# Values loaded by GpSimd's queue with the cast in the transfer, and causal masks two blocks at a time

## The chip, the cores and the metric

The kernel runs on one core of a Trainium2 chip. The core has a matrix engine (TensorE, PE in the profile; its weight loads are PEld), VectorE (DVE), ScalarE (ACT), GpSimd (POOL) and SyncE (SP), which here only issues transfers. Every engine works through its own instructions in program order and waits on semaphores for the others. Sixteen DMA engines move data between memory and the core's buffer; a transfer is issued by an instruction in the queue of SP, ACT or POOL. The metric is the device time of one execution in microseconds (us).

## The reference

The program is selective attention followed by a block with layer norm and a two-layer network. There are 8 batches, 8 heads, 576 positions, 64 elements per head.

```python
scores = scale * q @ k.T                       # per batch and head, 576 x 576
cum = cumsum(max(s, 0))                        # per batch and head
scores = where(causal, -1e9, scores + minimum(-(cum[i] - cum[j]), 0))
attn = softmax(scores)
x = attn @ v                                   # heads side by side: (8, 576, 512)
xn = (x - mean) / sqrt(var + 1e-6) * g_ln
out = x + max(xn @ w_ch1, 0) @ w_ch2           # 512 -> 2048 -> 512
```

All inputs are float32 in memory, and so is the output.

## The kernel before

The work is a sequence of 64 heads, numbered n = 8 b + h over batch b and head h. The 576 positions are cut into four tiles of 128 and one of 64. For each head, `scores` (L344) computes transposed score blocks on PE into three banks, sa, sb and sc; ACT takes the exponential of each bank into the tile `er` (four heads deep, in bfloat16). The 64 x 64 corner blocks of two heads are done together in `scores_d` (L381). From head 10 on, the causal mask is applied on POOL after the exponentials: `affine_select` (L371) zeroes one half of each of the four 128 x 128 diagonal blocks of a head, and one more (L401) does the corners of two heads. `pv` (L419) then multiplies the masked exponentials with the values, 15 matmuls into the bank `pot`. The values lie in `v_bf`, two buffers that batches take in turns, with a column of ones that gives the sum of each row; `pv_norm` divides by it on DVE.

Between these, PE runs the two-layer network of the previous batch in units of four matmuls (`mlp1`, L533, and `mlp2`, L551), taken from a list (`queue`) by `run_units`. The first 18 heads are ordered by a written list of steps (`PLAN`, L946); from head 18 on a loop (L974) does, for every n: `pre(n)`, `scores`, units, `scores_d` for even heads, units, then `pv` of head n-2, then more units. So the pot of a head runs two heads later than its scores.

`pre(n)` (L852) holds the loads for later heads. Keys and queries are taken in groups of four heads (gam, two per batch). From group 5 on, `ld_rows` (L187) issues two loads per tile on SP's queue into a staging tile; `cast_rows` (L200) casts that tile on POOL and copies the bias columns; `tr_rows` (L210) issues a DMA transpose on SP's queue into `kq`, from which PE reads. For a group these steps come six to three heads ahead of its first head. The staging tiles (pool `stage`, six buffers) are shared by the row tiles and the value tiles.

Values of batches 0 and 1 are loaded by POOL's queue in the prologue, straight into `v_bf`, with the cast from float32 to bfloat16 in the transfer (`ld_cast_v`, L173). For batches 2 to 7, `pre(n)` calls `ld_v` (L162), which loads one tile of v in float32 into a staging tile on SP's queue, and one head later `cast_v` (L180), which casts it on POOL into `v_bf`. For batch nb the five tiles are loaded at heads n = 8 nb - 7 to 8 nb - 3 (for batch 2: 11 to 15) and cast one head later. Within `pre(n)` the value steps come behind the steps for rows, and the masks of head n come behind `pre(n)` on POOL. The weights (`w1_bf`, `w2_bf`) and the pairs of keys and queries of early groups also come by POOL's queue, in the prologue and at heads 11 and 12. Finished rows of the output are stored by SP's queue at the end of a `mlp2` quarter.

Of the kernel before, what the change touches and what calls it, by code (L numbers as in the profile page):

```python
# [9 lines left out]
F32 = mybir.dt.float32  # L10
# [5 lines left out]
P = 128  # L16
# [3 lines left out]
def kernel(  # L20
# [11 lines left out]
    nc = tc.nc  # L32
    B, H, S, D = q.shape
# [5 lines left out]
    NF = S // P  # L39
    NT = NF + 1  # L40
    TL = S - NF * P
# [3 lines left out]
    OB, OC, OD = 512, 1024, 1536  # L45
# [11 lines left out]
    stage = ctx.enter_context(tc.tile_pool(name="stage", bufs=6))  # L57
# [25 lines left out]
    v_bf = [const.tile([P, NT, H, D + 1], BF16, name=f"v_bf{i}") for i in range(2)]  # L83
# [27 lines left out]
    def copy_on(eng, out, in_):  # L111
        if eng == "act":
            nc.scalar.copy(out=out, in_=in_)
        elif eng == "dve":
            nc.vector.tensor_copy(out=out, in_=in_)
        else:
            nc.gpsimd.tensor_copy(out=out, in_=in_)  # L117


    loaded = {}  # L120
# [37 lines left out]
    def ld_cast_pair(g):  # L158
        ld_cast("k", g)
        ld_cast("q", g)  # L160

    def ld_v(b, t):  # L162
        if b >= B:
            return
        pn = P if t < NF else TL
        tmp = stage.tile([P, H, D], F32, name="vtmp", tag="st")
        nc.sync.dma_start(
            out=tmp[:pn], in_=v[b, :, t * P : t * P + pn, :].rearrange("h s d -> s h d")
        )
        loaded["v", b, t] = tmp  # L170


    def ld_cast_v(b, t):  # L173
        pn = P if t < NF else TL
        nc.gpsimd.dma_start(
            out=v_bf[b % 2][:pn, t, :, 0:D],
            in_=v[b, :, t * P : t * P + pn, :].rearrange("h s d -> s h d"),
        )

    def cast_v(b, t, eng):  # L180
        if b >= B:
            return
        pn = P if t < NF else TL
        copy_on(eng, v_bf[b % 2][:pn, t, :, 0:D], loaded.pop(("v", b, t))[:pn])


    def ld_rows(gam, t):  # L187
        pn = P if t < NF else TL
# [39 lines left out]
    def ld_w2(i):  # L228
        nc.gpsimd.dma_start(
            out=w2_bf[:, 4 * i : 4 * i + 4, :], in_=w2_r[:, 4 * i : 4 * i + 4, :]  # L230
        )
# [89 lines left out]
    def k_cols(b, h, kb):  # L321
        i, hh = home(b * 2 + h // G), h % G
        if b * 2 + h // G < NPE:
            return kq[i][0:KA, 0, hh, kb * P : (kb + 1) * P]
        n = P if kb < NF else TL
        o = kb * 2 * G * P + hh * n
        return kq[i].rearrange("p u h s -> p (u h s)")[0:KA, o : o + P]

    def q_cols(b, h, q0, q1):
        i, hh = home(b * 2 + h // G), h % G  # L330
        if b * 2 + h // G < NPE:
            return [(q0, q1, kq[i][0:KA, 1, hh, q0:q1])]
        flat = kq[i].rearrange("p u h s -> p (u h s)")
        full = flat[0:KA, 0 : NF * 2 * G * P].rearrange("p (t h s) -> p t h s", t=NF, s=P)
        o = NF * 2 * G * P + (G + hh) * TL
        got = []
        if q0 < NF * P:
            qf = min(q1, NF * P)
            got.append((q0, qf, full[:, q0 // P : qf // P, G + hh, :]))
        if q1 > NF * P:  # L340
            got.append((NF * P, q1, flat[0:KA, o : o + TL]))
        return got

    def scores(b, h):  # L344
        e = er[:, h % 4, :]
        pe_mask = b * H + h < NM

        def bank(name, blocks, o):
            a = ps_s.tile([P, 512], F32, name=name, tag="s")
            for c, kb, q0, q1, diag in blocks:  # L350
                for a0, a1, cols in q_cols(b, h, q0, q1):
                    nc.tensor.matmul(  # L352
                        a[:, c + a0 - q0 : c + a1 - q0],
                        lhsT=k_cols(b, h, kb),
                        rhs=cols,
                        start=True,
                        stop=not (pe_mask and diag),
                    )
                if pe_mask and diag:
                    nc.tensor.matmul(  # L360
                        a[:, c : c + P], lhsT=ident, rhs=maskT, start=False, stop=True
                    )
            nc.scalar.activation(out=e[:, o : o + 512], in_=a, func=ACT.Exp, scale=scale)  # L363

        bank("sa", ((0, 0, 0, 512, True),), 0)
        bank("sb", ((0, 0, 512, 576, False), (64, 1, 128, 576, True)), OB)
        bank("sc", ((0, 2, 256, 576, True), (320, 3, 384, 576, True)), OC)
        if pe_mask:
            return
        for o in (0, OB + 64, OC, OC + 320):  # L370
            nc.gpsimd.affine_select(  # L371
                out=e[:, o : o + P],
                in_=e[:, o : o + P],
                compare_op=ALU.is_ge,
                fill=0.0,
                base=0,
                pattern=[[1, P]],
                channel_multiplier=-1,
            )

# [79 lines left out]
    st = {}  # L460
# [168 lines left out]
    for i in range(2):  # L629
# [9 lines left out]
        out=maskT,  # L639
        in_=maskT,  # L640
# [3 lines left out]
        pattern=[[1, P]],  # L644
# [207 lines left out]
    def pre(n):  # L852
        if n == 14:
            for r in rows:
                nc.gpsimd.memset(r[:, :, :, KA:P], 0.0)
        if n in PAIR_LOADS:
            ld_cast_pair(PAIR_LOADS[n])
        if n in (11, 12):
            ld_w2(n - 9)
        if n in (8, 9):  # L860
            aug(n - 5, nc.sync)
        for gam in range(NPE, NG):
            m = n - 4 * gam
            if m == -6:
                ld_rows(gam, 0), ld_rows(gam, 1)
            elif m == -5:
                cast_rows(gam, 0), cast_rows(gam, 1)
                ld_rows(gam, 2), ld_rows(gam, 3)
            elif m == -4:
                tr_rows(gam, 0), tr_rows(gam, 1)  # L870
                cast_rows(gam, 2), cast_rows(gam, 3)
                ld_rows(gam, 4)
            elif m == -3:
                tr_rows(gam, 2), tr_rows(gam, 3)
                cast_rows(gam, 4)
                tr_rows(gam, 4)
        for nb in range(2, B):
            m = n - H * nb + (5 if nb == 2 else 7)
            if 0 <= m < NT:
                ld_v(nb, m)  # L880
            if 1 <= m <= NT:
                cast_v(nb, m - 1, "pool")

    def pv_next():
        pb, ph_ = pend.pop(0)
# [4 lines left out]
        if ph_ == 7:  # L890
# [8 lines left out]
            out=c_in[:, 0:P], in0=c_in[:, 0:P], scalar=0.0, in1=eight, op0=ALU.max, op1=ALU.mult  # L899
# [24 lines left out]
            out=c_in[:, P:S], in_=c_in[:, P:S], func=ACT.Relu, scale=1.0 / scale  # L924
# [16 lines left out]
        "U": lambda: run_units(1, True),  # L941
        "u": lambda: run_units(1),
        "p": lambda n: pre(n),
    }

# [21 lines left out]
    for word in PLAN.split():  # L967
        step, _, eng = word.partition(":")
# [5 lines left out]
    for n in range(2 * H + 2, BH):  # L974
        b, h = n // H, n % H
# [65 lines left out]
```

## Time and profile before

| | |
|---|---|
| median of three runs | 362.97 us (362.14 to 363.56) |
| the profiled execution, its own time | 361.1 us |
| its span (first to last instruction) | 359.4 us |
| PE busy | 348.9 us, 97% |
| DVE, ACT, POOL busy | 199.1, 187.5, 169.6 us |
| masks on POOL (L371) | 216 instructions, 59.0 us |
| casts of v on POOL (L117) | 30 instructions, 18.3 us |
| casts and copies of rows on POOL (L204, L205) | 110 instructions, 45.0 us |
| v loads issued on SP (L167) | 30, median 596 ns to issue |
| v loads issued on POOL in the prologue (L175) | 10, median 928 ns to issue |
| read from memory, written to it | 37.11 MB, 9.44 MB |

How to read the views. A row of a group gives a line of the kernel, an engine, an operation, output and inputs by name, their shapes, how many there were, their busy time and the mean length of one, and how long the engine sat idle just before them, with what ended most of that. In a view in order of time, a line gives the start in us, the length, the engine, and the same names; instructions of one kind that follow each other are merged (x15), and a bracket tells how long the engine idled before and what released it. A view by stretches gives, for each stretch, the busy time of PE, PEld, DVE, ACT and POOL with their instruction counts, PE's granted clock, the mean busy share of the DMA engines and the GB/s that they moved. Matmuls are pipelined, so their lengths overlap; the step from one group's start to the next is the time that PE gives to it. An instruction that issues a transfer counts as no busy time of its engine in the page's first row.

### The profile page before, as it was taken

The page shows a single profiled execution, that of the slowest core. Times are in us where ns is not written, and L with a number is a line of the kernel's source. Part 1 is how long each engine was busy: PE and PEld are TensorE (multiplying, and loading weights), DVE is VectorE, ACT ScalarE, POOL GpSimd, SP SyncE. Part 2 cuts the span into 40 slices and gives each one's busy share as a digit, 9 for nine tenths or more (in the row PEclk, how much of TensorE's full clock was granted, in tenths as well). Part 3 has the DMA queues.
Part 4 walks back from the last instruction along what each step waited for, and adds up shares of the span by engine and source line. Part 5 has one row for each costly group of instructions (what it writes and reads, how often), then busy time and mean ns, then how long its engine had stood idle before and what let it go on. Part 6 is the DMA issues. An engine that isn't in the chain of part 4 may idle for free.

```text
span 359.4 us, 8530 instructions
## 1 busy us (share of the span) xinstructions
PE 348.9 (97%) x3144; PEld 200.8 (56%) x3190; DVE 199.1 (55%) x540; ACT 187.5 (52%) x363; POOL 169.6 (47%) x451
## 2 busy tenths in 40 slices
PE   7999999989999999999999999999999999999995
PEld 3899665545555555555555555555555554444444
DVE  7787888924476536844484539543855482113111
ACT  4899886557524763367326743575247432501500
POOL 9996768456666562464745473537422110000000
PEclk9999999999999999999999999999999999999999
DMA  9999999999899998599889885999610011011013
GB/s 151 173 186 172 201 196 202 184 215 210 183 161 257 201 167 176 143 208 178 187 194 206 193 179 116 247 170 182 139 60 2 2 58 59 2 58 58 0 33 88
DMA packets 164202, 52.09 MB, mean 145 GB/s; under 512 B 152848, under 2 KB 159552, under 8 KB 164160
## 3 DMA queue, kind: packets, MB, share of 16 engines
q1 hardware_dynamic: 139248, 42.43, 56.3%
q0 software_dynamic: 23472, 8.33, 20.6%
q10 hardware_dynamic: 1440, 0.79, 0.9%
q8 instruction: 25, 0.41, 0.5%
q14 instruction: 17, 0.14, 0.1%
HBM read 37.11 MB, written 9.44 MB: 130 GB/s over the span
## 4 chain that ended last, share of the span: by engine, by line
PE 85%; DVE 5%; DMA 3%; POOL 2%; issue 2%; SPq 1%; POOLq 0%; DVEq 0%
PE ph L537 32%; PE py L555 27%; PE pot L429 6%; PE sc L352 3%; PE sb L352 3%; PE sa L352 3%; PE ph L817 2%; PE trx L522 2%; PE st L715 2%; DMA rowtmp<-in_q_dram 2%; DVE xn L504 2%; PE pot L773 1%; PE trt L693 1%; DMA c_in<-in_s_dram 1%; DMA kq<-kq 1%
## 5 line engine op out<-in xcount | busy, mean ns | idle before, releaser
L555 PE MATMUL py<-w_bf,hT 128*128 128x512 bf16 (+1 forms) x565 | 132.5, 373 | 1.5 <-DVE yo L564 0.4
L537 PE MATMUL ph<-xT,w_bf 128*128 128x512 bf16 x462 | 113.0, 379 | 1.1 <-DVE yo L564 0.2
L547 ACT ACTIVATE hT<-ph 128x512 bf16<-128x512 f32 x100 | 59.6, 597 | 65.2 <-PE ph L537 65.2
L555 PEld LDWEIGHTS <-hT 128*128 128x128 bf16 x592 | 53.4, 98 | 48.8 <-issue 0.9
L537 PEld LDWEIGHTS <-w_bf 128*128 128x128 bf16 x544 | 48.6, 97 | 49.9 <-issue 2.9
L363 ACT ACTIVATE er<-sa 128x512 bf16<-128x512 f32 x56 | 33.4, 596 | 66.0 <-PE sa L352 42.1
L371 POOL TENSOR_SCALAR_AFFINE_SELECT er<-er 128x128 bf16<-128x128 bf16 x216 | 59.0, 298 | 18.6 <-ACT er L363 18.4
L545 DVE TENSOR_SCALAR hT<-ph 128x512 bf16<-128x512 f32 x36 | 24.9, 692 | 58.2 <-PE ph L537 57.9
L204 POOL CAST kq<-rowtmp 128x512 bf16<-128x512 f32 (+1 forms) x55 | 33.4, 606 | 38.3 <-DMA rowtmp<-in_q_dram 37.7
L352 PEld LDWEIGHTS <-kq 68*128 68x128 bf16 x412 | 29.9, 97 | 22.4 <-issue 0.5
L429 PEld LDWEIGHTS <-er 128*128 128x128 bf16 x840 | 33.0, 98 | 13.7 <-POOL er L371 1.5
L564 DVE SCALAR_TENSOR_TENSOR yo<-py,rstd,xb 128x512 f32<-128x512 f32 x32 | 24.0, 749 | 24.4 <-PE py L555 17.9
L441 DVE RECIPROCAL rinv<-pot 128x5 f32<-128x5 f32 x56 | 10.7, 191 | 48.1 <-PE pot L429 47.9
L429 PE MATMUL pot<-v_bf,er 128*128 128x65 bf16 x840 | 35.3, 194 | 1.1 <-POOL er L371 1.0
L363 ACT ACTIVATE er<-sc 128x512 bf16<-128x512 f32 x56 | 34.3, 613 | 0.0
L117 POOL CAST v_bf<-vtmp 128x512 bf16<-128x512 f32 (+1 forms) x30 | 18.3, 612 | 32.4 <-DMA vtmp<-in_v_dram 24.6
L363 ACT ACTIVATE er<-sb 128x512 bf16<-128x512 f32 x56 | 33.6, 600 | 0.0
L443 DVE TENSOR_TENSOR xb<-pot,rinv 128x256 f32<-128x256 f32 x56 | 23.8, 425 | 1.9
L483 POOL TENSOR_TENSOR rstd<-rstd,mhalf 128x4 f32<-128x4 f32 (+1 forms) x8 | 8.7, 1091 | 32.7 <-DVE rstd L482 32.7
L504 DVE SCALAR_TENSOR_TENSOR xn<-xb,mv,gb 128x512 bf16<-128x512 f32 x28 | 21.9, 783 | 1.0
L467 DVE BATCH_NORM_STATS2 stats<-xb 128x6 f32<-128x128 f32 (+1 forms) x84 | 21.9, 320 | 0.3
L352 PE MATMUL sc<-kq 68*128 68x256 bf16 (+1 forms) x200 | 21.7, 226 | 0.0
(117 smaller groups left out, 372.6 us busy)
## 6 DMA issues: line engine op xcount, KB each, us to landing
out_dram<-yo SPq DMA_DIRECT2D x32, 256.0 KB
vtmp<-in_v_dram SPq DMA_DIRECT2D x24, 256.0 KB
rowtmp<-in_k_dram SPq DMA_DIRECT2D x44, 128.0 KB
rowtmp<-in_q_dram SPq DMA_DIRECT2D x44, 128.0 KB
w_bf<-in_moe_w_ch_dram POOLq DMA_DIRECT2D x8, 512.0 KB, 9.4
v_bf<-in_v_dram POOLq DMA_DIRECT2D x8, 128.0 KB, 6.2
kq<-kq SPq DMA_TRANSPOSE x55
kp<-in_k_dram POOLq DMA_DIRECT2D x6, 144.0 KB, 8.8
```

What stands on the lines that cost most here:

```text
L204: nc.gpsimd.tensor_copy(out=r[0:pn, :, :, 0:D], in_=loaded.pop(("rows", gam, t))[0:pn])
L352: nc.tensor.matmul(a[:, c + a0 - q0 : c + a1 - q0], lhsT=k_cols(b, h, kb), rhs=cols, start=True, stop=not (pe_mask and diag),)
L363: nc.scalar.activation(out=e[:, o : o + 512], in_=a, func=ACT.Exp, scale=scale)
L371: nc.gpsimd.affine_select(out=e[:, o : o + P], in_=e[:, o : o + P], compare_op=ALU.is_ge, fill=0.0, base=0, pattern=[[1, P]], channel_mult ...
L429: nc.tensor.matmul(pot[:, t, :], lhsT=e[:, o : o + P], rhs=vv[:, kb, h, :], start=(kb == 0), stop=(kb == last),)
L443: nc.vector.tensor_tensor(out=xb[b][:, :, hs], in0=pot[:, 0:NF, 0:D], in1=rinv[:, 0:NF].unsqueeze(2).to_broadcast([P, NF, D]), op=ALU.mult,)
L504: nc.vector.scalar_tensor_tensor(out=xn, in0=tiles[t], scalar=mvs[b][:, t, 0:1] if b > 0 else mean0[:, t : t + 1], in1=gb, op0=ALU.subtrac ...
L537: nc.tensor.matmul(ph, lhsT=w1_bf[:, kd, fb * P : (fb + 1) * P], rhs=xT[:, kd, :], start=(kd == 0), stop=(kd == KD - 1),)
L545: nc.vector.tensor_scalar_max(out=hT[:, fb, :], in0=ph, scalar1=0.0)
L547: nc.scalar.activation(out=hT[:, fb, :], in_=ph, func=ACT.Relu)
L555: nc.tensor.matmul(py[t], lhsT=hT[:, fb, t * P : (t + 1) * P], rhs=w2_bf[:, fb, c0:c1], start=(fb == 0), stop=(fb == FB - 1),)
L564: nc.vector.scalar_tensor_tensor(out=yo, in0=py[t], scalar=rs, in1=x[:, c0:c1], op0=ALU.mult, op1=ALU.add)
```

## The change

The value tiles of batches 2 to 7 no longer pass through a staging tile. `pre(n)` issues their loads on POOL's queue, with the cast in the transfer, two tiles at n = 8 nb - 4 and three at n = 8 nb - 3, by the function that the prologue uses. `ld_v` and `cast_v` go. The four masks of a head become two instructions, each over two diagonal blocks: blocks 0 and 1, which lie 576 columns apart, and blocks 2 and 3, which lie 320 apart.

```diff
-    def ld_v(b, t):
-        if b >= B:
-            return
-        pn = P if t < NF else TL
-        tmp = stage.tile([P, H, D], F32, name="vtmp", tag="st")
-        nc.sync.dma_start(
-            out=tmp[:pn], in_=v[b, :, t * P : t * P + pn, :].rearrange("h s d -> s h d")
-        )
-        loaded["v", b, t] = tmp
...
     def ld_cast_v(b, t):
         pn = P if t < NF else TL
         nc.gpsimd.dma_start(
             out=v_bf[b % 2][:pn, t, :, 0:D],
             in_=v[b, :, t * P : t * P + pn, :].rearrange("h s d -> s h d"),
         )
-
-    def cast_v(b, t, eng):
-        if b >= B:
-            return
-        pn = P if t < NF else TL
-        copy_on(eng, v_bf[b % 2][:pn, t, :, 0:D], loaded.pop(("v", b, t))[:pn])
...
-        for o in (0, OB + 64, OC, OC + 320):
+        for o, step in ((0, OB + 64), (OC, 320)):
+            two = e[:, o : o + 2 * step].rearrange("p (i c) -> p i c", c=step)[:, :, 0:P]
             nc.gpsimd.affine_select(
-                out=e[:, o : o + P],
-                in_=e[:, o : o + P],
+                out=two,
+                in_=two,
                 compare_op=ALU.is_ge,
                 fill=0.0,
                 base=0,
-                pattern=[[1, P]],
+                pattern=[[0, 2], [1, P]],
                 channel_multiplier=-1,
             )
...
         for nb in range(2, B):
-            m = n - H * nb + (5 if nb == 2 else 7)
-            if 0 <= m < NT:
-                ld_v(nb, m)
-            if 1 <= m <= NT:
-                cast_v(nb, m - 1, "pool")
+            for t in {-4: (0, 1), -3: (2, 3, 4)}.get(n - H * nb, ()):
+                ld_cast_v(nb, t)
```

## The prediction

> **What bounds the kernel now.** I read the busy shares first, then the span in forty slices, then busy time by stretches of 10 us, then the order of time of PE, POOL and SP where a stretch stood out, and last the waits. The page:
>
> ```profile
> PE 348.9 (97%) x3144; PEld 200.8 (56%) x3190; DVE 199.1 (55%) x540; ACT 187.5 (52%) x363; POOL 169.6 (47%) x451
> PEclk9999999999999999999999999999999999999999
> L117 POOL CAST v_bf<-vtmp 128x512 bf16<-128x512 f32 (+1 forms) x30 | 18.3, 612 | 32.4 <-DMA vtmp<-in_v_dram 24.6
> L371 POOL TENSOR_SCALAR_AFFINE_SELECT er<-er 128x128 bf16<-128x128 bf16 x216 | 59.0, 298 | 18.6 <-ACT er L363 18.4
> ```
>
> PE is busy 97% at full clock; 10.5 us of the 359.4 us span are left. An edit on POOL and on the queues takes no work from PE, so it can win only what PE idles, and lose what it makes PE wait. The stretches tell where the idling is:
>
> ```profile
> 0.00:10.00 10.00, 8.09 (x49) 3.72 (x50) 7.29 (x28) 5.25 (x10) 9.25 (x18) 1.00 1.38 152
> ...
> 60.00:70.00 10.00, 9.89 (x88) 5.68 (x89) 9.37 (x25) 6.94 (x14) 7.18 (x19) 1.00 1.04 195
> 70.00:80.00 10.00, 8.69 (x83) 4.89 (x83) 4.13 (x12) 5.37 (x12) 4.41 (x12) 1.00 0.93 208
> 80.00:90.00 10.00, 9.95 (x87) 5.37 (x85) 4.30 (x12) 7.45 (x16) 6.77 (x22) 1.00 1.02 212
> ```
>
> The second number is PE's busy time. Start-up (8.09) and the last stretch (the final output) are out of the change's reach; 70 to 80 is the one stretch in the middle that falls short. There, PE and then POOL in order of time:
>
> ```profile
> 72.53 0.38 PE L352 MATMUL sa<-kq 68*128 68x512 bf16 x1
> 73.11 0.38 PE L352 MATMUL sb<-kq 68*128 68x64 bf16 x3 [0.20 <-DMA kq<-kq]
> ...
> 74.48 1.03 PE L537 MATMUL ph<-xT,w_bf 128*128 128x512 bf16 x4
> 76.50 1.24 PE L429 MATMUL pot<-v_bf,er 128*128 128x65 bf16 x15 [0.99 <-POOL er L371]
> 77.58 1.89 PE L537 MATMUL ph<-xT,w_bf 128*128 128x512 bf16 x7
> ```
>
> ```profile
> 68.48 0.20 POOL L205 COPY kq<-cT 64x32 bf16<-64x32 bf16 x1
> 75.59 0.61 POOL L117 CAST v_bf<-vtmp 128x512 bf16<-128x512 f32 x1 [6.91 <-PE ph L537]
> 76.16 1.03 POOL L371 TENSOR_SCALAR_AFFINE_SELECT er<-er 128x128 bf16<-128x128 bf16 x4
> ```
>
> This is head 18. Its exps ended at 66.1, yet its four masks ran at 76.16, because the first v cast of batch 3 stood ahead of them on POOL. The cast is put down to PE, but its load was issued on SP only at 71.58, behind three transposes (67.24, 4.29 us); the load is the likelier releaser. Steps between PE's groups give the cost. From sa to sb is normally 0.22 us (68.15 to 68.37), here 0.58: 0.36 lost. Four matmuls from 74.48 take 0.86, so pot could start at 75.34 and started at 76.50: 1.16 lost. From pot to the next group is 0.46 elsewhere (81.69 to 82.15), here 1.08: 0.62 lost. Together **2.14 us**. Everywhere else in the middle PE is within 0.3 us of full in every 10 us.
>
> **Part 1: the v path leaves SP and the casts leave POOL.** Off SP go 30 issues of 0.596 us (the median of their row), 17.9 us of a queue that also carries row loads, transposes and output. Off POOL go 24 casts of 613 ns and 6 of 606 ns, 18.3 us, with 24.6 us of waiting for their loads. The staging buffers are then shared by the row tiles alone, so SP's short waits for v casts (0.9 and 0.8 us in all) go too. For batch 2 the three v loads issued at 36.00 disappear ahead of the row loads of group 5, whose first issue took 9.79 us on SP (40.12 to 49.91). These rows come earlier, and so do the transposes behind the 0.36 us wait.
>
> **Part 2: 30 loads are issued on POOL.** The ten v loads of batches 0 and 1 are the same instruction: mean 0.89 us, 0.70 to 0.96, five in a row in 4.24 us. 24 whole ones at 0.89 and 6 half ones at 0.70 are 25.6 us, 7.3 us more than the casts. They come in two bursts per batch, two ahead of the masks of head 8b-4 (1.8 us) and three ahead of those of head 8b-3 (2.5 us), each behind the row casts of that head. Nothing in either burst waits for a load: v_bf's other user, batch b-2, made its last pot three heads earlier. The pot of head h runs two heads later, so there is cover. Behind the end of the last row copy I put 2.5 us of issues and 0.7 us of masks, and compare with the pot in the trace. Head 29: 123.99+3.2=127.2 against 128.63, 1.4 us free. Head 37: 162.30+3.2=165.5 against 166.95, 1.5. Head 45: 199.31+3.2=202.5 against 204.68, 2.2. Head 53: 238.67+3.2=241.9 against 243.00, 1.1. At heads 8b-4 there is more (head 28: masks end at 119.4, pot at 124.06). So I cost the bursts at nothing from batch 4 on; if the cover goes, each further us costs one us per batch.
>
> The bound for the data: in the packet records a 256-byte packet of SP's queue takes 21.3 ns in the mean, a 128-byte one written by a casting load 34. A whole v load is 1024 packets on 16 engines, so 1.36 us becomes 2.2 us of engine time, 22 us over the 27 whole-load equivalents, against a mean DMA share near 0.9 from 60 to 260 us. It lands 5.1 to 8.2 us after issue in the first batches; the first pot of a batch comes five heads, over 20 us, later. For batch 2 the margin is thinner: issues end at about 56, landing by 64.2, first pot at 66.38. None of it is on the path, by these rows.
>
> The Trainium skill has a rule against this part: SBUF — State Buffer, "The DVE blocks DMA trap (SWDGE)", says GpSimd cannot write descriptors while VectorE runs a 2-port perf-mode operation, and its example goes from about 620 to 3100 ns. The ten issues here took at most 0.96 us, five of them between 23.78 and 28 with DVE 81% busy, so the row is taken. By the page's example, as an estimate, each issue would cost 2.5 us more, the burst of three 7.4 us, and the change would be slower by some 5 us in each of five batches.
>
> **Part 3: two masks in one.** 216 instructions become 108. From below, an operation of twice the elements costs no more than one now (286 ns); from above, twice that. POOL's cast and copy rows give a slope: 206 ns for 32 elements, 608 for 512, 0.84 ns per element. So 286+107=393 ns, and 59.0 us become 42, nearer to the lower bound. The first mask now waits for the second exp too, 0.48 us after the first; in the middle POOL reaches the masks after all exps are done. At the end of the heads it waits for exps (L371's 18.4 us of idling), but the pot of head 63 starts at 285.96, masks done by 281.2. Worth nothing by itself on PE; it pays POOL for Part 2 (POOL in all 169.6-18.3+25.6-17=160 us).
>
> **The sum.** The mask wait at head 18 goes altogether (nothing stands ahead of those masks but row 4's copy at 68.48): 1.78. The 0.36 goes with the earlier rows. What is late next is batch 3: PE comes 2.14 us sooner to heads 19 to 24, while rows of group 6 are still loaded in the old order. Row 4's load was issued at 83.51 behind four v issues (0.57, 0.51, 0.45, and 0.61 after it) and POOL's late casts at 78.56; I find it 2 us earlier, its cast at 84.9, three issues to 88.1, masks at 88.8, and pot of head 21 wanted at 88.76. That is no margin: 0 to 0.6 us back, I take 0.3. Net gain 1.8 us. The profiled execution took 361.1 us (span 359.4 and 1.7 around it), which becomes 359.3. It lies 1.9 below the median of the three runs, 362.97, so the median becomes **361.2**; its own range is 360.6 to 362.2.
>
> **Rivals.** A: the stall moves to batch 3 or to the transposes. The last transpose of group 6 left SP at 90.26 and is needed at 93.08, or 90.9 once PE is early; if the chain of rows does not move, 1 to 2 us come back. For it: every step of the chain is a DMA of 2 to 4 us. Against it: it loses 2.3 us of SP issues and POOL's wait. Time: 361.4 to 363.0.
>
> B, on the other side: row 4's load is slowed by the casting loads issued just ahead of it, its cast holds POOL, three issues follow, and the masks of head 8b-3 come late in each batch. The delay can be from below nothing (v no longer precedes it on SP's queue) to 4.4 us (two whole loads at 34 ns ahead of every packet). With margins of 1.4, 1.5, 2.2 and 1.1 us it cancels the gain from a delay of 2.0 us and costs 0.5% beyond it at 2.5; 3 us gives 5.8-1.8=4.0 us lost, 367. For it: a DMA share of 0.9, and SP issues that stretched to 9.79 us while POOL's weight loads ran. Against it: the row load is 512 packets only.
>
> C: the loads are hidden and the mask is no cheaper; the stall goes still, since it comes from order, not from durations; then 361.2 to 361.8.
>
> **How the numbers follow.** The forecast, with C in it, has 0.50, A 0.25, B 0.25. About 0.5% (1.8 us) is what a measurement can tell from no change, and the forecast sits at that edge; most of what I left out (the 0.3) leans to the faster side, so 0.42 faster; the rest of the forecast and A give 0.33 same; B 0.25 slower. The range runs from the full gain with a little more, 360.3, into B, 365.0.
>
> **What would show it.** Right: PE busy about 9.9 in the stretch 70 to 80, no pot waiting for L371, no POOL wait for vtmp, POOL's v issues at 0.85 to 0.95 us, masks near 0.39. Wrong: pot waiting for L371 at heads 21, 29, 37, 45 or 53 (B), sa or sb waiting for kq's transposes near 91 (A), issues over 1.3 us (the skill's rule), PE busy below 9.7 in stretches that were at 9.9.

## The result, and the profile after

The changed kernel takes 360.77 us (median of 20 executions, 359.27 to 363.62) against 362.73 us for the kernel before (20 executions, 360.05 to 363.83). The ratio is **0.996, with a 95% interval of 0.9944 to 0.9976**: 0.9 to 2.0 us faster, a small gain that is clear of zero, and less than the 0.5% that was called distinguishable. The ratios in this document lie nearer to the quotient of the means (here 0.9957, 1.6 us) than to that of the medians (0.9946, 2.0 us). The prediction was 361.2 us. A second set of 12 executions beside three experiments gave 361.24 us and a ratio of 0.9948 (0.9922 to 0.9974). Ratios count executions in the fast state alone, which are all but four of f1's twelve.

The profiled execution took 360.48 us, its span is 358.4 us; before it was 361.1 and 359.4. So the two profiled executions differ by 1.0 us of span, and this is the difference that their traces can explain. The page of after:

```profile
PE 350.8 (98%) x3190; PEld 200.6 (56%) x3190; DVE 200.1 (56%) x540; ACT 187.4 (52%) x363; POOL 162.1 (45%) x343
q1 hardware_dynamic: 111120, 35.35, 52.0%
q0 software_dynamic: 51600, 11.87, 37.4%
L186 POOL CAST kq<-rowtmp 128x512 bf16<-128x512 f32 (+1 forms) x55 | 34.0, 618 | 78.1 <-DMA rowtmp<-in_q_dram 56.6
L354 POOL TENSOR_SCALAR_AFFINE_SELECT er<-er 128x256 bf16<-128x256 bf16 x108 | 42.9, 423 | 21.2 <-ACT er L345 20.8
L164 POOL DMA_DIRECT2D v_bf<-in_v_dram x40 | 34.3, 869 | 0.4 <-issue 0.3
```

Line numbers moved up: the masks are L354, the row casts L186, the transposes L196, the v loads L164, pot L412, the scores L334. PE's 350.8 us against 348.9 mean nothing by themselves: the trace of before lacks 46 matmul records (3144 of 3190), that of after lacks none. POOL has 162.1 us of busy time (predicted 160), and the masks of two blocks take 423 ns in the mean. On POOL the profile does count an instruction that issues a transfer as busy: the 162.1 us hold the 34.3 us of v issues. The packets of 30 v loads moved from SP's queue (q1, 139248 before) to POOL's (q0, 23472 before), and q0 now holds the 16 DMA engines for 37.4% of the span, where it was 20.6%. POOL idles 78.1 us ahead of row casts, 56.6 of them put down to the row loads that its row names; before it was 38.3 us, and 37.7 of them.

The stretches, with PE's busy time as the second number:

```profile
70.00:80.00 10.00, 10.00 (x107) 5.93 (x106) 4.92 (x13) 7.18 (x15) 4.66 (x11) 1.00 0.85 202
80.00:90.00 10.00, 9.31 (x79) 4.74 (x76) 4.30 (x12) 7.02 (x14) 7.58 (x15) 1.00 1.41 163
```

The hole of 70 to 80 (8.69) is closed. A smaller one has opened in 80 to 90 (9.31, was 9.95). PE in order of time, around heads 18 and 21:

```profile
72.55 0.38 PE L334 MATMUL sa<-kq 68*128 68x512 bf16 x1
72.77 0.38 PE L334 MATMUL sb<-kq 68*128 68x64 bf16 x3
...
75.00 0.61 PE L412 MATMUL pot<-v_bf,er 128*128 128x65 bf16 x15
...
87.05 1.89 PE L520 MATMUL ph<-xT,w_bf 128*128 128x512 bf16 x8
89.61 0.83 PE L412 MATMUL pot<-v_bf,er 128*128 128x65 bf16 x15 [0.67 <-POOL er L354]
90.27 1.89 PE L520 MATMUL ph<-xT,w_bf 128*128 128x512 bf16 x8
```

The loop runs the pot of a head in the step that computes the scores of the head two later, so the sa and sb beside the pot of head 18 are those of head 20, the first of group 5; "at head 18" means this step, here and below. At head 18 sb follows sa by 0.22 us (0.58 before) and pot starts at 75.00 without a wait (76.50 before): all of the 2.14 us came back. At head 21 eight matmuls from 87.05 take 1.73 us at full pace, so pot was wanted at 88.78 and started at 89.61: 0.83 us late. From pot to the next group is 0.66 us in place of 0.46: 0.20 more, while the masks of that head still ran beside it. So 1.03 us went again, and 2.14 - 1.03 = 1.1 us is close to the 1.0 us between the spans. The chain of waits shows what held head 21 (start, length, what):

```profile
81.77 4.03 DMA rowtmp<-in_q_dram
...
85.94 0.60 POOL kq L186
86.54 0.15 POOL kq L187
86.70 2.43 POOL v_bf L164 x3
89.12 0.43 POOL er L354
89.56 0.05 issue
89.61 0.33 PE pot L412 x5
```

Row 4 of group 6 was loaded late; behind its cast stand the three v issues, behind those the masks. The issues of that load on SP and two casting loads on POOL stand at the same time; the kernel before follows behind the dots:

```profile
81.01 1.84 POOL L164 DMA_DIRECT2D v_bf<-in_v_dram  x2 [0.35 <-issue]
81.77 0.61 SPq L174 DMA_DIRECT2D rowtmp<-in_q_dram  x1
85.94 0.60 POOL L186 CAST kq<-rowtmp 64x512 bf16<-64x512 f32 x1 [2.07 <-DMA rowtmp<-in_q_dram]
...
84.44 0.61 SPq L192 DMA_DIRECT2D rowtmp<-in_q_dram  x1
86.96 0.60 POOL L204 CAST kq<-rowtmp 64x512 bf16<-64x512 f32 x1 [2.10 <-DMA rowtmp<-in_q_dram]
```

SP had finished issuing that load at 82.38; the cast started at 85.94, 3.6 us later. In the kernel before the same step took from 85.05 to 86.96, 1.9 us.

### The profile page after: what moved, and what is told of

The parts are those of the page before. It is cut to its first block, busy times and chain, and to the rows that moved or that the text cites. A ratio compares the mean times of both kernels' runs of the same rounds, so it can differ in the third digit from the quotient of the medians.

```text
span 358.4 us, 8434 instructions
## 1 busy us (share of the span) xinstructions
PE 350.8 (98%) x3190; PEld 200.6 (56%) x3190; DVE 200.1 (56%) x540; ACT 187.4 (52%) x363; POOL 162.1 (45%) x343
## 3 DMA queue, kind: packets, MB, share of 16 engines
q0 software_dynamic: 51600, 11.87, 37.4%
## 4 chain that ended last, share of the span: by engine, by line
PE 83%; DVE 6%; DMA 3%; POOL 2%; SPq 2%; issue 1%; ACT 1%; POOLq 0%; DVEq 0%; ACTq 0%
PE ph L520 30%; PE py L538 30%; PE pot L412 6%; DMA rowtmp<-in_q_dram 3%; PE sc L334 3%; PE sb L334 3%; PE sa L334 3%; PE ph L800 2%; SPq L174 2%; DVE xn L487 2%; PE trx L505 2%; PE st L698 2%; PE pot L756 1%; PE trt L676 1%; POOL kq L186 1%
## 5 line engine op out<-in xcount | busy, mean ns | idle before, releaser
L538 PE MATMUL py<-w_bf,hT 128*128 128x512 bf16 (+1 forms) x592 | 136.7, 373 | 0.7 <-DVE yo L547 0.7
L186 POOL CAST kq<-rowtmp 128x512 bf16<-128x512 f32 (+1 forms) x55 | 34.0, 618 | 78.1 <-DMA rowtmp<-in_q_dram 56.6
L354 POOL TENSOR_SCALAR_AFFINE_SELECT er<-er 128x256 bf16<-128x256 bf16 x108 | 42.9, 423 | 21.2 <-ACT er L345 20.8
L334 PEld LDWEIGHTS <-kq 68*128 68x128 bf16 x412 | 29.9, 97 | 22.0
L412 PEld LDWEIGHTS <-er 128*128 128x128 bf16 x840 | 32.8, 98 | 13.2 <-POOL er L354 1.2
L412 PE MATMUL pot<-v_bf,er 128*128 128x65 bf16 x840 | 34.9, 194 | 0.7 <-POOL er L354 0.7
L164 POOL DMA_DIRECT2D v_bf<-in_v_dram x40 | 34.3, 869 | 0.4 <-issue 0.3
L345 ACT ACTIVATE er<-sc 128x512 bf16<-128x512 f32 x56 | 34.3, 613 | 0.0
L487 DVE SCALAR_TENSOR_TENSOR xn<-xb,mv,gb 128x512 bf16<-128x512 f32 x28 | 23.0, 820 | 1.0
L334 PE MATMUL sc<-kq 68*128 68x256 bf16 (+1 forms) x200 | 21.7, 226 | 0.1
```

Source lines behind the costliest of these rows:

```text
L164: nc.gpsimd.dma_start(out=v_bf[b % 2][:pn, t, :, 0:D], in_=v[b, :, t * P : t * P + pn, :].rearrange("h s d -> s h d"),)
L186: nc.gpsimd.tensor_copy(out=r[0:pn, :, :, 0:D], in_=loaded.pop(("rows", gam, t))[0:pn])
L334: nc.tensor.matmul(a[:, c + a0 - q0 : c + a1 - q0], lhsT=k_cols(b, h, kb), rhs=cols, start=True, stop=not (pe_mask and diag),)
L354: nc.gpsimd.affine_select(out=two, in_=two, compare_op=ALU.is_ge, fill=0.0, base=0, pattern=[[0, 2], [1, P]], channel_multiplier=-1,)
L412: nc.tensor.matmul(pot[:, t, :], lhsT=e[:, o : o + P], rhs=vv[:, kb, h, :], start=(kb == 0), stop=(kb == last),)
L487: nc.vector.scalar_tensor_tensor(out=xn, in0=tiles[t], scalar=mvs[b][:, t, 0:1] if b > 0 else mean0[:, t : t + 1], in1=gb, op0=ALU.subtrac ...
```

## The experiments

All times are medians of 12 executions; the kernel before, run beside them, had 362.78 (e), 362.91 (f) and 362.70 us (g; 35 executions each). "Lost at head 18" and the like are worked out as in the prediction: steps between PE's groups less the same step without a wait (0.22 us from sa to sb, 2.00 from the pot before to sa, 0.46 from pot to the next group).

### First: which part brings it

**e1: the kernel before with the masks in pairs, v as before.**

```diff
-        for o in (0, OB + 64, OC, OC + 320):
+        for o, step in ((0, OB + 64), (OC, 320)):
+            two = e[:, o : o + 2 * step].rearrange("p (i c) -> p i c", c=step)[:, :, 0:P]
...
-                pattern=[[1, P]],
+                pattern=[[0, 2], [1, P]],
```

> The kernel before with only the masks two at a time; v still comes by SP and a cast on POOL. Theory (what costs is the order on POOL: a v cast that waits for its load stands ahead of the masks of head 18): the stall at head 18 stays, since the masks are late in starting, not long; pot there still waits about 1 us for the mask, the masks take 0.42 us each and 43 us in all, and the time is that of before within 0.3 us (gain 0 to 0.3 us). Rival (POOL's busy time counts, 16 us less of it are felt): a gain of 1 us or more.

362.3 us, ratio 0.9985 (0.9966 to 1.0004). POOL is busy for 153.7 us instead of 169.6. PE waits at head 18 much as before (1.76 us lost), and once more at head 22, for the transposes of group 6 (1.07 us lost), where the trace of before has no wait:

```profile
73.50 0.38 PE L352 MATMUL sb<-kq 68*128 68x64 bf16 x3 [0.32 <-DMA kq<-kq]
...
76.80 0.84 PE L430 MATMUL pot<-v_bf,er 128*128 128x65 bf16 x15 [0.90 <-POOL er L372]
...
94.39 0.40 PE L352 MATMUL sb<-kq 68*128 68x64 bf16 x3 [0.90 <-DMA kq<-kq]
```

What POOL gains, 16 us, is worth nothing measurable: at head 18 POOL is idle before the v cast, and shorter masks behind it start no earlier (76.34, before 76.16).

**e2: the changed kernel with its four masks per head.** The masks block of the diff is undone; the v path stays changed.

> The changed kernel with four masks per head again; v by POOL's queue. Theory (order): the whole of the change's gain is here. Head 18 has no wait. At head 21 pot starts up to 0.1 us earlier than in the changed kernel (the first mask is done after 0.29 us, not 0.41), but the fourth is done 0.3 us later, so the loss there is 1.0 to 1.4 us; the time is that of the changed kernel within 0.4 us, a ratio of 0.995 to 0.998 to before. Rival (the pairing of masks is what keeps POOL on time in all batches): waits for masks at several heads, and a time as before or above.

359.88 us, ratio 0.9941 (0.9918 to 0.9964), span 357.1. The gain is in the v path: this interval and e1's do not touch. PE waits neither at head 18 nor at head 21, where row 4's cast starts at 84.50 and not at 85.94. The load took 3.3 us to its cast, nearly as long as in the changed kernel, but SP had issued it 1.2 us earlier (81.17 against 82.38). The masks cost more POOL time here and head 21 is on time, so in this execution the wait was decided by when the row load lands and not by the length of the masks.

### Second: is it the order on POOL

**e3: the kernel before, with the v casts of batches 3 to 7 behind the masks of their head.** Loads stay on SP.

```diff
             if 0 <= m < NT:
                 ld_v(nb, m)
-            if 1 <= m <= NT:
+            if 1 <= m <= NT and n < 2 * H + 2:
                 cast_v(nb, m - 1, "pool")
...
+        casts_behind(n)          # the same cast_v, called behind scores, ahead of scores_d
```

> The kernel before with one thing moved: from head 18 on the v cast of a head is issued on POOL behind the four masks of that head, not ahead of them. Loads, casts and masks are all as before. Theory (order): masks of head 18 run at about 69 us, pot waits for nothing there, 1.8 us come back and PE is near 9.9 in the stretch from 70 to 80; the sum is at least that of the changed kernel, a gain of 1.4 to 2.1 us (ratio 0.994 to 0.996), with no casting transfer at all. Rival (it is the route: freed SP queue, freed staging tiles): the stall shrinks by less than 0.5 us and the time is that of before.

361.93 us, ratio 0.9983 (0.9963 to 1.0003). The wait for masks at head 18 is gone, so the prediction's reading of it was right. In this trace PE waits for the DMA transposes of the rows instead:

```profile
73.88 0.38 PE L352 MATMUL sa<-kq 68*128 68x512 bf16 x1 [0.30 <-issue]
74.95 0.38 PE L352 MATMUL sb<-kq 68*128 68x64 bf16 x3 [0.69 <-DMA kq<-kq]
...
94.80 0.38 PE L352 MATMUL sa<-kq 68*128 68x512 bf16 x1 [1.19 <-DMA kq<-kq]
95.42 0.39 PE L352 MATMUL sb<-kq 68*128 68x64 bf16 x3 [0.24 <-DMA kq<-kq]
```

The last two lines are rival A of the prediction, in the form "the chain of rows does not move". My theory that order alone brings the gain fell: the median shows none. Why is not settled by this one trace. It was late before the edit acts, which is from head 18 on: the last three transposes of group 5 start at 68.88 there and at 67.24 before, so the first two waits are not the edit's doing. Those of group 6 start 2.1 us later than before (88.33 against 86.25), so part of the last two waits is the same lateness carried on.

**f1: the same, and the v loads of batches 3 to 7 on SP three heads later.** The offset of 7 heads in `pre` becomes 4; casts behind the masks as in e3.

```diff
-            m = n - H * nb + (5 if nb == 2 else 7)
+            m = n - H * nb + (5 if nb == 2 else 4)
```

> The kernel before with the v casts behind the masks, and for batches 3 to 7 the v loads on SP, and their casts, three heads later (heads 8b-4 to 8b). v still goes by SP, staging tile and cast. With the casts behind the masks alone, the mask wait of head 18 was gone, but PE then waited about 1.1 us for the transposes of group 5 (near 74 us) and 1.4 us for those of group 6 (near 94), and the ratio to before was 0.9983. Theory (the v loads of batch 3 ahead of the row loads of group 6 on SP's queue make those rows late; the freed queue is half of the change's gain): the wait near 94 goes or falls below 0.5 us, the one near 74 stays, since batch 2's loads stay where they were; ratio 0.994 to 0.997. Rival (the rows are late because of POOL or because transposes are slow by themselves): the wait near 94 stays at 1 us or more; ratio 0.997 to 1.000.

366.27 us over all twelve, 365.39 over the eight in the ratio, which is 1.0056 (1.0019 to 1.0093): slower. Its profiled execution (362.01 us) is the fastest of its twelve, so it shows a good case. Both transposes waits are gone (PE 9.89 in 70 to 80, 9.94 in 90 to 100). The theory had the one in 70 to 80 staying, since batch 2's loads stay where they were; that it went says that this wait differs from execution to execution. The price stands mainly in one line:

```profile
105.31 0.19 PE L429 MATMUL pot<-v_bf,er 128*128 128x65 bf16 x1 [2.12 <-POOL v_bf L117]
```

The first pot of batch 3 waits for the last v cast, and another pot does so for 0.62 us at 182.14. In these two traces with v on SP, either the rows come late (e3) or the values do. What the other executions lost beyond that, their traces would have to show, and there are none.

**g1 and g2: one half of the v path each.** g1 loads batch 2 alone by POOL, g2 batches 3 to 7 alone; masks are four in both.

```diff
         for nb in range(2, B):
+            if nb == 2:                 # g1; in g2: nb > 2
+                for t in {-4: (0, 1), -3: (2, 3, 4)}.get(n - H * nb, ()):
+                    ld_cast_v(nb, t)
+                continue
             m = n - H * nb + (5 if nb == 2 else 7)
```

> Only batch 2's v is loaded by POOL with the cast in the transfer; v of batches 3 to 7 goes by SP, vtmp and a POOL cast as before, and the masks are four. Theory (the 2.14 us at head 18 has two causes, the v cast of batch 3 ahead of the masks, and group 5's rows and transposes coming late behind batch 2's v loads): the rows of group 5 and their transposes come earlier, so no sa or sb of head 18 waits for kq, and the load of batch 3's first v tile, which stands behind those transposes on SP, comes earlier with them; the pot of head 18 waits for the masks under 0.5 us instead of 0.99; PE busy over 9.3 in 70 to 80; span 357.8 to 358.8 against 359.4. In 90 to 100 the transposes of group 6 may be waited for by up to 1 us, as SP still carries batch 3's v. Rival (the gain comes from batches 3 to 7 alone): the pot of head 18 still waits about 1 us for the masks, PE 8.7 in 70 to 80, span 359.4 or more.

g1: 361.85 us, ratio 0.9962 (0.9937 to 0.9987), span 359.6. In the profile it does what the rival said:

```profile
72.55 0.38 PE L352 MATMUL sa<-kq 68*128 68x512 bf16 x1
73.40 0.38 PE L352 MATMUL sb<-kq 68*128 68x64 bf16 x3 [0.48 <-DMA kq<-kq]
...
74.77 1.03 PE L537 MATMUL ph<-xT,w_bf 128*128 128x512 bf16 x4
76.58 1.24 PE L429 MATMUL pot<-v_bf,er 128*128 128x65 bf16 x15 [0.79 <-POOL er L371]
77.66 0.59 PE L537 MATMUL ph<-xT,w_bf 128*128 128x512 bf16 x2
```

Lost at head 18: 0.63 (sa to sb), 0.95 (pot wanted at 75.63), 0.62 (pot to the next group): 2.20 us, as before. SP's queue shows why the relief did not arrive:

```profile
59.20 4.76 SPq L214 DMA_TRANSPOSE kq<-kq  x2
...
67.35 4.27 SPq L214 DMA_TRANSPOSE kq<-kq  x3
71.67 0.57 SPq L167 DMA_DIRECT2D vtmp<-in_v_dram  x1
```

Group 5's first pair of transposes starts 1.7 us earlier than before (60.90) but takes 4.76 us instead of 3.71, beside batch 2's casting loads, and row 4's load behind it takes longer as well; the last three start at 67.35 (67.24 before). The profile therefore explains no gain of g1; the 0.4% of its median is left open.

> The other half: batch 2's v goes by SP, vtmp and a POOL cast as before, batches 3 to 7 by POOL with the cast in the transfer, in bursts of two and three; the masks are four. Theory: no mask wait at head 18, but sa and sb of head 18 wait for the transposes of group 5 by 0.7 to 1.2 us in all, as where the casts stood behind the masks (0.30 and 0.69); no wait for group 6's transposes near 94, since SP carries no v by then; the pot of head 21 late by 0 to 0.5 us, as PE comes to it later; PE 9.0 to 9.4 in 70 to 80; span 358.0 to 359.0. Rival (the earlier rows of group 5 are worth nothing): no wait for kq at head 18, span 357.1 as with all batches by POOL.

g2: 362.82 us, ratio 0.9991 (0.9961 to 1.0021), span 361.9. No wait for masks at head 18, a short one for transposes, a short one for batch 2's last cast, and a long one at head 21:

```profile
68.20 0.19 PE L429 MATMUL pot<-v_bf,er 128*128 128x65 bf16 x1 [0.43 <-POOL v_bf L117]
74.79 0.38 PE L352 MATMUL sb<-kq 68*128 68x64 bf16 x3 [0.32 <-DMA kq<-kq]
91.87 1.08 PE L429 MATMUL pot<-v_bf,er 128*128 128x65 bf16 x15 [0.92 <-POOL er L371]
```

The theory had the kind of the first loss right and its size wrong (0.48 us at head 18, not 0.7 to 1.2), it put head 21 at 0 to 0.5 us late where it was 1.08, and the span at 358.0 to 359.0. So in this kernel, too, the mask wait of head 18 is gone and the time is that of before. The intervals of the two halves overlap each other and that of the whole, so the times do not say which of them carries more.

### Third: what the casting loads do to the rows

**e4: the changed kernel, with the v issues behind the masks of their head.** The same `ld_cast_v` calls, moved behind `scores` and ahead of `scores_d` for batches 3 to 7.

> The changed kernel with one thing moved: from head 18 on the v loads of heads 8b-4 and 8b-3 are issued on POOL behind the masks of the head. Theory (the three issues, 2.48 us, between row 4's cast and the masks make the stall of 1.03 us at head 21): the masks of head 21 start at about 86.7 and end at 87.5, pot starts at 88.8 without a wait, and 1.0 us comes back: a ratio 0.003 below that of the changed kernel, 0.992 to 0.995 to before. Rival (the late landing of row 4, not the issues, or another wait takes its place at the transposes of group 6): less than 0.3 us comes back.

360.42 us, ratio 0.9942 (0.9914 to 0.997). No wait at head 21. The profiled execution (362.86 us, span 360.8) lost some 2 us in 30 to 40 us, ahead of anything that this edit touches, and waits at head 23 for masks that stand behind late row casts of group 7 (97.64, 99.94):

```profile
101.12 0.84 PE L412 MATMUL pot<-v_bf,er 128*128 128x65 bf16 x15 [0.75 <-POOL er L354]
```

So the order of issues and masks decides the 2.5 us between row 4's cast and the masks, but what it gives at head 21 it can lose two heads on. In the median nothing tells it from the change.

**f2: the changed kernel without the v loads of batches 3 to 7.** This leaves work out: the pots of those batches multiply with the values that batches 1 and 2 left in the two buffers.

```diff
         for nb in range(2, B):
+            if nb > 2:
+                continue
             for t in {-4: (0, 1), -3: (2, 3, 4)}.get(n - H * nb, ()):
```

> The changed kernel without any load of v for batches 3 to 7 (their pots use the values of batches 1 and 2). Theory (the casting loads slow row 4's load, and their issues stand between its cast and the masks): from the last issue of row 4's load of group 6 to its cast it takes about 2 to 2.5 us, not 3.6 as in the changed kernel; no pot waits for a mask; PE is full from 60 to 260; what the v loads still cost in the changed kernel is 0 to 1.0 us, so a ratio of 0.991 to 0.995 to before. Rival (row 4's load takes 3.5 us with or without them): the same 3.5 us.

359.65 us, ratio 0.9913 (0.9887 to 0.994), span 357.3, with nothing but 0.2 us lost at head 18. This is the floor: by the ratios, all that the v loads of batches 3 to 7 still cost in the changed kernel is (0.996 - 0.9913) x 363 = 1.7 us, or 1.3 us with the second ratio of 0.9948; the ends of the first two intervals allow 0.2 to 3.2 us. Row 4's load takes 1.8 us to its cast, less even than the 2 to 2.5 of the theory. The 1.03 us at head 21 is the part of it that a trace shows.

**f3: all five v loads of a batch one head later, at head 8 nb - 2,** which is after the last row load of the group.

```diff
-            for t in {-4: (0, 1), -3: (2, 3, 4)}.get(n - H * nb, ()):
+            at = {-4: (0, 1), -3: (2, 3, 4)} if nb == 2 else {-2: (0, 1, 2, 3, 4)}
+            for t in at.get(n - H * nb, ()):
```

> The changed kernel with the five v loads of batches 3 to 7 all issued at head 8b-2, ahead of its masks (batch 2 as it was). Theory (casting loads delay the row loads that run beside them, whichever those are): row 4 of group 6 is back at 2 to 2.5 us and head 21 has no wait, but the rows of group 7, loaded at head 22, come 2 to 3 us later than in the changed kernel (first casts there at 95.7 and 96.8), and the pot of head 23 waits 1 to 3 us for masks that stand behind those casts; smaller waits at heads 31, 39, 47. Ratio 0.996 to 1.003, slower than the changed kernel. Rival (rows take the same time wherever v is loaded): no wait at head 23, ratio 0.992 to 0.995.

360.45 us, ratio 0.9931 (0.9903 to 0.996). No wait at head 21; row 4's load takes 2.1 us from issue to cast. No wait at head 23 came either, so the theory fell there, though the casting loads did slow the rows of group 7 that were now loaded beside them: the first two transposes take 4.25 us (2.66 before), and a row cast waits 3.45 us for its load.

```profile
95.84 4.25 SPq L196 DMA_TRANSPOSE kq<-kq  x2
96.61 0.61 POOL L186 CAST kq<-rowtmp 128x512 bf16<-128x512 f32 x1 [3.45 <-DMA rowtmp<-in_q_dram]
```

What PE still waits for is at head 18, the transposes of group 5, which batch 2's loads stand beside and which this edit leaves alone:

```profile
73.09 0.38 PE L334 MATMUL sa<-kq 68*128 68x512 bf16 x1 [0.40 <-DMA kq<-kq]
74.08 0.38 PE L334 MATMUL sb<-kq 68*128 68x64 bf16 x3 [0.61 <-DMA kq<-kq]
```

**f4: one v load per head, from head 8 nb - 6 to 8 nb - 2.** The same `at`, with `{t - 6: (t,) for t in range(NT)}`.

> The changed kernel with the v loads of batches 3 to 7 one per head, at heads 8b-6 to 8b-2, ahead of the masks (batch 2 as it was). Theory (it is the burst that costs: 2.48 us of issues at one place and three casting loads beside one row load): no head has more than 0.9 us of issues ahead of its masks, no row load is beside more than one casting load, and neither head 18 nor 21 nor 23 waits; ratio 0.991 to 0.995, at or below the changed kernel. Rival (any casting load beside the rows delays them, so five places instead of two): waits of 0.3 to 1 us at several heads, ratio 0.995 to 1.000.

362.7 us, ratio 0.9997 (0.9965 to 1.0029). No gain is left to see, which is what the rival said. The rows of a group now meet a casting load at several places: row 4's load takes 4.6 us from issue to cast, the last three transposes of group 6 take 4.91 us together (3.80 before), and PE waits for transposes three times:

```profile
73.14 0.38 PE L334 MATMUL sb<-kq 68*128 68x64 bf16 x3 [0.22 <-DMA kq<-kq]
92.05 0.39 PE L334 MATMUL sb<-kq 68*128 68x64 bf16 x3 [0.34 <-DMA kq<-kq]
```

The third is 0.72 us near 245.3; the first is group 5's, which this edit leaves alone. One load per head is slower than one burst of five at head 8 nb - 2 (f3): the two intervals do not touch. From the changed kernel itself f4 is not told apart.

**g3: all five v loads at head 8 nb - 3, ahead of the masks,** none at 8 nb - 4: more issues ahead of the masks, but no casting load beside row 4's load. The same `at`, with `{-3: (0, 1, 2, 3, 4)}`.

> The changed kernel with all five v loads of batches 3 to 7 issued ahead of the masks of head 8b-3, none at head 8b-4. Theory (row 4's load of group 6 takes 3.6 instead of 2 us because two casting loads were issued just ahead of it): row 4's load finds no casting load, its cast on POOL comes at 84.3 to 85.0, five issues of 0.87 end at 89.3, the masks' first at 89.7, and the pot of head 21, wanted at 88.8, is late by 0.7 to 1.4 us, so the two extra issues about cancel what the load gains; span 358.2 to 359.2 against 358.4, and later batches show the wait at head 8b-1 by up to 0.7 us where their margin was 0.8 to 1.0. Rival (only the order on POOL counts, the load's 3.6 us is not from the casting loads): cast at 85.9 as before, issues to 91.0, pot of head 21 late by 2.5 us, span about 360 and more.

361.52 us, ratio 0.9952 (0.9927 to 0.9976), span 358.1.

```profile
81.34 4.10 SPq L196 DMA_TRANSPOSE kq<-kq  x3
83.46 0.60 POOL L186 CAST kq<-rowtmp 64x512 bf16<-64x512 f32 x1 [2.64 <-DMA rowtmp<-in_q_dram]
84.58 4.28 POOL L164 DMA_DIRECT2D v_bf<-in_v_dram  x5 [0.36 <-issue]
88.82 1.52 POOL L354 TENSOR_SCALAR_AFFINE_SELECT er<-er 128x256 bf16<-128x256 bf16 x4
...
89.34 0.83 PE L412 MATMUL pot<-v_bf,er 128*128 128x65 bf16 x15 [0.36 <-POOL er L354]
```

With two more issues (1.8 us) ahead of them the masks start earlier, not later, than in the changed kernel (88.82 against 89.11), and pot is 0.53 us late instead of 0.83. The rival, order alone, wanted 2.5. Row 4's cast comes 2.5 us earlier than in the changed kernel (83.46 against 85.94): 1.15 us because SP had issued the load earlier (81.23 against 82.38), and 1.3 us because it took 2.2 us instead of 3.6. In e2 SP issued it at the same time as here (81.17), with two casting loads beside it, and the cast came at 84.50, 1.0 us later. So row 4's load was held up by the two casting loads issued beside it.

**g4: the changed kernel once more,** beside g1 to g3.

> The changed kernel once more, beside the three kernels above. Theory: span 358 to 359, PE without a wait at head 18; the pot of head 21 late by 0 to 1 us, since by the rows of the kernels beside it that wait is on the edge. Rival (the late pot at head 21 is fixed by the order of work): 0.8 to 0.9 us late again, to 0.1 us.

361.24 us, ratio 0.9948 (0.9922 to 0.9974); its profiled execution has 361.85 us and a span of 360.1, and shows something else than the first trace of the same kernel:

```profile
73.44 0.38 PE L334 MATMUL sa<-kq 68*128 68x512 bf16 x1 [0.46 <-DMA kq<-kq]
74.38 0.38 PE L334 MATMUL sb<-kq 68*128 68x64 bf16 x3 [0.56 <-DMA kq<-kq]
91.02 0.83 PE L412 MATMUL pot<-v_bf,er 128*128 128x65 bf16 x15 [0.47 <-POOL er L354]
```

sa comes 2.62 us after the pot before it instead of 2.00, sb 0.94 after sa instead of 0.22: 1.3 us lost at head 18, to the transposes of group 5, whose first pair took 5.59 us this time (4.40 in the first trace). Head 21 then loses 0.84. The masks are not waited for at head 18 in any of the traces where v of batch 3 goes by POOL. The theory (no wait at head 18 at all) fell with this run.

### The rows of all kernels together

The last three transposes of group 6 (the three lengths on SP's queue added) and row 4's load of that group (end of its issue on SP to its cast on POOL), by whether casting loads were issued at head 20, or spread over the heads before, so that they run beside them. The lengths are added one by one because a merged x3 line also holds the time between the three. In the changed kernel the third transpose starts at 86.72, when the copy behind row 4's cast is done, and the line of all three would say 5.43 us, part of it this wait:

| no casting load beside them | before | e1 | e3 | f1 | f2 | f3 | g1 | g3 |
|---|---|---|---|---|---|---|---|---|
| three transposes, us | 3.80 | 3.82 | 3.86 | 3.83 | 3.76 | 3.73 | 3.74 | 3.77 |
| row 4, issue to cast, us | 1.9 | 1.8 | 2.1 | 2.0 | 1.8 | 2.1 | 1.8 | 2.2 |

| casting loads beside them | after | e2 | e4 | g2 | g4 | f4 |
|---|---|---|---|---|---|---|
| three transposes, us | 4.72 | 5.21 | 4.27 | 5.29 | 5.24 | 4.91 |
| row 4, issue to cast, us | 3.6 | 3.3 | 3.4 | 4.0 | 3.6 | 4.6 |

The two groups do not overlap. The first pair of transposes of group 5 shows the same beside batch 2's loads, less sharply: 2.80 to 4.03 us in the five kernels that load batch 2 on SP, 3.93 to 5.59 in the nine that load it by POOL. And the first pair of group 7, which in f3 and g3 stands beside the burst of five, takes 4.25 and 4.58 us there, 2.66 before and 2.62 to 2.87 in ten others; f1, with v on SP, has 3.53.

## Why the prediction was right, point by point

- **What bounds the kernel, and the 2.14 us.** Right. PE has no free work to give; the one hole was head 18's, and it closed. That the v cast ahead of the masks caused the mask wait in it (1.78) is shown from both sides: e3 and g2 move the cast or remove it, and the mask wait goes; g1 and e1 keep it, and the wait stays (1.57 and 1.29 us of it). That 1.78 us of time comes back with it is not shown: e3 and g2 have no such wait, and neither is measurably faster than before. The whole v path together is (e2).
- **"The 0.36 goes with the earlier rows."** Right in the first trace, not in g4, where 1.3 us went to the same transposes. SP's row issues do come earlier, by 2.1 us at the first pair of transposes (58.81 against 60.90), but only 0.6 us of that is left at the last three (66.68 against 67.24). About half of the loss is the pair itself, 4.40 us instead of 3.71 beside batch 2's casting loads; most of the rest is output stores that took 1.76 us instead of 1.01, whose cause is open. The working counted the issues that leave SP's queue and took nothing for this. Over all traces the wait at this place runs from nothing to 1.3 us with batch 2's v on SP (f1, e3) and from nothing to 1.3 with it on POOL (after, g4).
- **Part 2, the issues.** Right: 40 at 869 ns in the mean (0.89 and 0.70 predicted for the two kinds). The bursts of three took 2.5 us as predicted, and the longest of the 40 issues 0.975 us. The Trainium skill's example (SBUF — State Buffer, "A bandwidth-pool intuition that's wrong (but worth ruling out)") goes to about 3100 ns. No issue here came near that; whether VectorE ran an operation of the kind that the page names beside one of them, no run here shows. "Nothing from batch 4 on" was right too: at heads 29, 37, 45 and 53 the masks that pot needs were done 1.6, 0.8, 1.0 and 2.4 us ahead of it (1.4, 1.5, 2.2 and 1.1 predicted).
- **Part 3, the masks.** 423 ns instead of 393; two in a row step by 0.36, where one of before steps by 0.25. Worth nothing by itself, as said, and as e1 shows.
- **"What is late next is batch 3, head 21."** The right head, the right chain, the wrong size: 0.3 us taken (0 to 0.6), 1.03 measured. The term that was mis-sized is row 4's cast, put at 84.9. The load was issued 2.7 us earlier than before, more than the 2 us assumed, but took 3.6 us to the cast instead of 1.9, so the cast came at 85.94. Two casting loads were issued beside it, from 81.01 to 82.85. That is the mechanism of rival B, priced there at 0 to 4.4 us of delay: it is real and measures 1.7 us. It costs time only at head 21, because at the later heads the margins hold. B put the gain at nothing from a delay of 2.0 us, but it added up the four later heads and left out head 21, where the sum had no margin. Two of the prediction's own signs of being wrong came: a pot that waits for masks at head 21, and PE below 9.7 in a stretch that was at 9.9 (9.31 in 80 to 90).
- **Rival A** (the transposes become the next wait) is what e3, g4, f3 and f4 show at one place or another, 0.4 to 1.3 us each time at head 18. In the first trace of the changed kernel it is absent. e1, which has the v path of before, loses 1.07 us to it at head 22, so it is not brought by the change alone.
- **Rival C** did not hold: the masks are cheaper. It made no difference.
- **The sum.** The profile was to go from 361.1 to 359.3 and went to 360.48; the median was to be 361.2 and is 360.77. The first misses by the 0.7 us at head 21 and by 0.4 us more that lie outside the span (2.1 around it instead of 1.7; in the medians of the executions 1.97 and 1.72). The second was reached by adding the 1.9 us by which the profiled execution of before lay under its median; that of after lies only 0.3 under its own. The two errors, 1.2 and 1.6 us, go opposite ways, so that the median came within 0.4 us is in part luck. Traced losses between 60 and 100 us are 2.14, 2.20 and 2.83 where the v cast of batch 3 stands ahead of the masks (before, g1, e1), and 1.03, 2.18 and about 0 with the whole v path changed (after, g4, e2): 1.3 us between their means. By the ratios the executions gained 1.5, 1.9 and 2.1 us (after, g4, e2). Single times of one kernel spread by some 4 us and one trace is one draw; where the executions gain the rest stays open.

No version was shown to beat the change: the intervals of e2 (0.9941), f3 (0.9931), e4 (0.9942) and g3 (0.9952) all overlap its own. By f2 some 1.3 to 1.7 us was left to gain from where these loads stand, within the wide margin given there.

## What to carry to other kernels

When an engine is 97% busy, look for the one place where it is not, and follow the wait there back through the queues: a cheap instruction that waits for a late load, in front of masks that others need, made the one hole of the trace, and 108 masks saved made no measurable difference. Then ask what is late next once that wait is gone; here it was, within a microsecond, the row loads and their transposes. Undoing the wait alone, by order (e3) or by moving the loads of batches 3 to 7 (g2), brought nothing measurable; moving all six batches did, and moving batch 2 alone (g1) gave 0.4% that its trace does not explain. A transfer that leaves a queue does not leave the DMA engines: price the loads and transposes that will run beside it in its new place, and put it where those have time to spare.

## What the runs showed that I had not expected

A casting load from POOL's queue slows the transfers of SP's queue beside it: three transposes from 3.8 to 4.7 us, a load of a row tile of 64 positions from 1.9 to 3.6 us from issue to cast, and the mean 256-byte packet of SP's queue from 22.0 ns (f2, which issues the same transfers on SP) to 24.5 (after). Moving the loads does not take this away: the packet means are 24.3, 25.0 and 24.8 ns in f3, g3 and f4. Packed into one burst (f3, g3) they slow the rows of group 7 in place of row 4 of group 6, where no pot waits for it; spread out (f4), they slow rows at more places, and PE waits at two of them. No run has a load on POOL's queue without the cast, so whether the cast or only the second queue slows the others is open.
